# A mixture-of-experts kernel: the second layer's input is cleared as float32 words on two engines, not as float16 on one

## The chip, the cores and the metric

The kernel runs on one core of a Trainium2 chip. The metric is the device time of one execution in microseconds (us); lower is better. Of the engines, TensorE is called PE in the profile, VectorE DVE, ScalarE ACT, GpSimd POOL, and the queue that issues most DMAs SP.

## The reference, cut to what matters

Three stages follow each other: a linear attention over 4 batches, 8 heads, 768 positions and head size 48; a layer of 8 experts (384 to 1024 to 384) that takes each of the 3072 tokens to the one expert with the largest logit; and a second, dense layer (384 to 2048 to 384).

```python
for t in range(S):                      # attention
    state = alpha[:, :, t, :, None] * state + np.einsum('bhd,bhe->bhde', k[:, :, t], v[:, :, t])
    y[:, :, t] = np.einsum('bhd,bhde->bhe', q[:, :, t], state)
...
for e in range(E):                      # the experts
    mask = expert_idx == e
    h = np.maximum(x[mask] @ w1[e], 0.0)
    out[mask] = gate_w[mask, None] * (h @ w2[e])
...
h = x @ w_in                            # the second layer
g = np.maximum(0.01 * h, h)
return (g @ w_out).astype(np.float32)
```

## The kernel before

Float32 products are made of float16 parts: a value is kept as hi + lo, and a product takes three matmuls (hi·hi, hi·lo, lo·hi).

**Attention and routing** fill the first 235 us. The last thing they do is to scatter the tokens' rows, 128 at a time, into a bucket of rows for each expert in HBM. These scatters are indirect DMAs that POOL issues at L558; the last six leave one after the other, the last at 235.07 us.

**The experts' stage** begins where the attention's pools are closed. Its buffers take the same places in SBUF as those of the attention, so the first instruction that writes to one of them waits until the attention's readers are through, the scatters included (they read the tile `xb`). Two of the new buffers, `x2h` and `x2l`, are the float16 parts of the second layer's input, each [128 partitions, 3, 3504], that is 10,512 float16 numbers on a partition. The experts write their results into them at places that are known only at run time (`ds(ao, CAP)`), each expert 432 columns wide, so both are cleared first:

```python
big = ctx.enter_context(tc.tile_pool(name="big", bufs=1))
x2h = big.tile([P, KD, X2], F16, name="x2h")
x2l = big.tile([P, KD, X2], F16, name="x2l")
nc.gpsimd.memset(x2h, 0.0)          # L698
nc.gpsimd.memset(x2l, 0.0)          # L699
```

The first write of an expert into `x2h` is ACT's at L908, that into `x2l` DVE's at L909, both at the end of the expert's work.

**Expert 0** needs its up to 432 rows as columns. The order of the instructions on each engine is that in which the code emits them. SP fetches the rows from the bucket in four blocks of 128, 128, 128 and 48 (`gather(0)`, L823), then four pieces of weights (L707 and L119), then the rows of expert 1 in two DMAs (`gather(1)`, L820 and L823). The four blocks are then scaled row by row, blocks 0 and 2 on DVE (L744), 1 and 3 on ACT (L742); PE transposes each block in three pieces (L750) into PSUM, and ACT and DVE write the float16 parts of the columns (L70 hi, L71 lo):

```python
def unit_rows(pool, xg, m, on_act=False):               # L738
    xs = pool.tile([P, D], F32, name="xs", bufs=3)
    if on_act:
        nc.scalar.activation(xs[:m], xg[:m, :D], AF.Copy, scale=xg[:m, D:D + 1])
    else:
        nc.vector.tensor_scalar(xs[:m], xg[:m, :D], xg[:m, D:D + 1], None, op0=ALU.mult)
    return xs
...
gather(0)                                               # in the experts' stage
ahead(0)
gather(1)
block_rows(0, 0)                                        # unit_rows on DVE
block_rows(0, 1)                                        # unit_rows on ACT
for n in range(NB):
    if n + 2 < NB:
        block_rows(0, n + 2)
    block_columns(0, n)                                 # L750, L70, L71
```

The matmuls of expert 0 begin with L758 and take all four blocks' columns at once (432). While expert e is computed, the rows of expert e+1 are made ready (L842 and L843, turned to columns by a DMA of ACT's queue, L849), and the weights of expert e+1 and a share of the second layer's are fetched and split into float16 parts (fetches L119 and L707 on SP; the stages on ACT L125, L127, L717 and L723; on DVE L132, L718 to L721 and L725; on POOL L130). The weights of expert 0 were split during the attention.

**The second layer** follows from 519 us on: 6 blocks of 512 tokens, PE busy nearly all the time.

Of the kernel before, what the change touches and what calls it, by code (L numbers as in the profile page):

```python
# [10 lines left out]
F16 = mybir.dt.float16  # L11
F32 = mybir.dt.float32
# [11 lines left out]
NP = H // 2          # head pairs  # L24
NC = S // P          # chunks of a sequence
D = H * HD           # 384
NT = B * S           # 3072 tokens
TT = NT // P         # 24 token tiles
W = P + 1            # a chunk's columns with its pad
AW = NC * W + 1  # L30
KD = D // P          # 3
E, F1, F2 = 8, 1024, 2048
NF1, NF2 = F1 // P, F2 // P
CAP = 432            # tokens of one expert in the static path
NB = -(-CAP // P)
AUG = D + 4          # a bucket row: x, scale in, scale out, token, token
NONE = 4096.0        # no token
CH = 768             # columns of a weight piece
W64 = 384            # of float64
# The engines run in the order of emission: one string for each pair of heads, one letter  # L40
# for each step, as the match statements in body() read them. LAST: the last pair and the
# tokens of the last batch.
# [19 lines left out]
BLK = 512            # columns of one MoE2 block  # L62
NBLK = NT // BLK
X2 = NT + CAP
OVB = 32             # blocks of tokens past the static places, at most


def to_f16_pair(nc, hi, lo, src, scale):
    """hi + lo = scale * src, as float16 parts."""
    nc.scalar.activation(hi, src, AF.Copy, scale=scale)  # L70
    nc.vector.scalar_tensor_tensor(lo, src, scale, hi, op0=ALU.mult, op1=ALU.subtract)  # L71
# [3 lines left out]
def body(ctx, tc, qT, kT, aT, v, emb, tau, w1, w2, w_in, w_out, out):  # L75
# [13 lines left out]
    before = const.tile([P, P], F16, name="before")     # s < t  # L89
# [3 lines left out]
    em8 = const.tile([P, NC, E], F32, name="em8")       # e - 8  # L93
# [5 lines left out]
    row0 = const.tile([P, E], F32, name="row0")         # an expert's first row  # L99
    nc.gpsimd.iota(row0, [[NT, E]], base=0, channel_multiplier=0, allow_small_or_imprecise_dtypes=True)  # L100
    cnt = const.tile([P, E], F32, name="cnt")           # sums over partitions to the row after its last one
    nc.vector.tensor_scalar(cnt, row0, 1.0 / P, None, op0=ALU.mult)
    enT = const.tile([P, KD, E], F32, name="enT")
    n_e = const.tile([P, E], F32, name="n_e")           # tokens of the experts
# [3 lines left out]
    more = []                                           # further pools of stages  # L108
# [36 lines left out]
    class Jobs:  # L145
        """Conversions of weights, each fetched some conversions ahead and done a stage at a time."""
# [9 lines left out]
        def step(self):  # L156
            """The next stage of those under way and the first of one more."""
            self.now = [g for g in self.now if next(g, self) is None]
            if self.got:
                convert, t = self.got.pop(0)  # L160
                g = convert(*t)
                next(g)
                self.now.append(g)
            self.fetch()
# [15 lines left out]
    with tc.tile_pool(name="awk", bufs=2) as awk, \  # L180
# [11 lines left out]
        mask = rt.tile([P, 4, P], F32, name="mask", bufs=1)      # s <= t  # L192
        nc.gpsimd.memset(mask, 1.0)
        nc.gpsimd.affine_select(mask, mask, [[0, 4], [1, P]], ALU.is_ge, 0.0, base=0, channel_multiplier=-1)
        # unit rows of the expert embedding, transposed
# [5 lines left out]
        def norm_of(dst, ssq, tmp, tmp2):  # L201
            """dst = sqrt(ssq): exp(ln / 2) and a Newton step."""
            nc.vector.tensor_scalar(tmp, ssq, 2.0 ** -60, None, op0=ALU.max)
            yield
            nc.scalar.activation(tmp, tmp, AF.Ln)
            nc.scalar.activation(tmp, tmp, AF.Exp, scale=0.5)
            yield 6
            nc.vector.reciprocal(tmp2, tmp)
            yield
            nc.vector.tensor_tensor(tmp2, tmp2, ssq, op=ALU.mult)  # L210
            yield
            nc.vector.tensor_tensor(tmp2, tmp2, tmp, op=ALU.add)
            yield
            nc.vector.tensor_scalar(dst, tmp2, 0.5, 1e-30, op0=ALU.mult, op1=ALU.max)
            yield
# [19 lines left out]
        def tick(at=None):  # L235
            """Two more steps of the chains of small operations; those for the tensor engine where it has the time."""
            for g in 2 * chains:
                if isinstance(g[1], int) and g[1]:
                    g[1] -= 1
                elif g[1] in (0, at):  # L240
                    g[1] = next(g[0], DONE) or 0
            chains[:] = [g for g in chains if g[1] != DONE]
# [9 lines left out]
        # rows that no token takes read as zeros; places without a token say so  # L252
# [16 lines left out]
        # the first two units bring what the rows between heads hold  # L269
# [20 lines left out]
        # one head of the pair each, zeros for the other: written where the head is, never elsewhere  # L290
        qzs = [rt.tile([P, NC, 2, P], F32, name=f"qz{i}", bufs=1) for i in range(2)]
        sts = [rt.tile([P, 2, HD * NC], F32, name=f"st{i}", bufs=1) for i in range(2)]
        # a chunk's whole product of alpha; before the first, none and no sum
# [6 lines left out]
        def prep(i):  # L300
            t = done[i]
            b, hp = units[i]
            if hp == 0:
                xbs[b] = awk.tile([P, NC, AUG], F32, name="xb", bufs=3)
            t.update({n: awk.tile([P, NC, 2 * HD], F16, name=n, bufs=3) for n in ("vh", "vl")})
            # products of alpha from its chunk's start, and one over them
            bc = t["bc"] = awk.tile([P, AW], F32, name="bc", bufs=2)
            nc.vector.tensor_tensor_scan(bc, t["a"], onesP, 0.0, op0=ALU.mult, op1=ALU.add)  # L308
            yield
            bcv = bc[:, 0:NC * W].rearrange("p (c w) -> p c w", w=W)  # L310
            nc.vector.reciprocal(seeds[:, W::W], bcv[:, :, P])
            t["qb"] = awk.tile([P, NC, P], F32, name="qb", bufs=4)
            nc.vector.scalar_tensor_tensor(t["qb"], t["q"].rearrange("p (c w) -> p c w", w=P), 16.0, bcv[:, :, 1:W], op0=ALU.mult, op1=ALU.mult)
            yield
            rc = awk.tile([P, AW], F32, name="rc", bufs=1)
            nc.vector.tensor_tensor_scan(rc[:, ::-1], t["a"][:, ::-1], seeds[:, ::-1], 0.0, op0=ALU.mult, op1=ALU.add)  # L316
            yield
            t["kh"] = awk.tile([P, NC, P], F32, name="kh", bufs=3)
            nc.vector.scalar_tensor_tensor(t["kh"], t["k"].rearrange("p (c w) -> p c w", w=P), 16.0,
                                           rc[:, 1:1 + NC * W].rearrange("p (c w) -> p c w", w=W)[:, :, 1:W], op0=ALU.mult, op1=ALU.mult)  # L320

# [4 lines left out]
        def values(i, eng=nc.gpsimd):  # L326
            """The pair's v, scaled, and its float16 parts."""
# [35 lines left out]
        def part(i, eng):  # L363
            """The float16 parts of the next of the masked scores."""
# [9 lines left out]
        def turns(*gs):  # L374
            """Steps of generators, one of each in turn."""
            gs = list(gs)
            while gs:
                gs = [g for g in gs if next(g, DONE) != DONE]
                tick()
# [29 lines left out]
        def combine(i, g):  # L409
            """Half of the chunks, in steps."""  # L410
# [52 lines left out]
        def last_columns(b, c0, n):  # L463
            """The last of the columns and logits of n tiles."""
# [9 lines left out]
        def scales(b, c0=0, n=NC):  # L474
            """The norms of the rows of n tiles, and what follows from them."""
            xb, cs, lo = xbs[b], slice(c0, c0 + n), 2 * (NP - 1) * HD
            ssq, t0, t1, nrm, ls, r = (rts[b][0][:, i, cs] for i in range(6))
            if n < NC:
                # the last pair's columns
# [15 lines left out]
        def route(b, scaled, c0=0, n=NC):  # L495
            """Experts, places and gates of the tokens in n tiles of batch b."""
# [14 lines left out]
            # the first expert that holds the maximum  # L511
# [15 lines left out]
            # an expert's first row and the tokens before this one at its expert  # L527
# [13 lines left out]
            # the gate: the largest probability  # L541
# [19 lines left out]
        with tc.manual_schedule():  # L561
# [9 lines left out]
            toward = []                         # tiles whose squares are to come  # L571
            for i in range(NU - 1):
                br, step = divmod(i - 5, NP)        # the batch whose tokens are routed
# [60 lines left out]
            # the last pair of heads and the last batch's tokens, by halves  # L634
# [63 lines left out]
    nc.gpsimd.memset(x2h, 0.0)  # L698
    nc.gpsimd.memset(x2l, 0.0)  # L699
# [10 lines left out]
    def convert_piece64(raw, hi, lo, n):  # L710
        """From the bits of float64: pairs of words, the low one first."""
# [4 lines left out]
        # 23 bits of the significand under the exponent less 896, then the sign (0 of a zero)  # L716
# [10 lines left out]
    def second_jobs(e):  # L727
        """This expert's share of the second layer's weights."""
# [9 lines left out]
    def unit_rows(pool, xg, m, on_act=False):  # L738
        """m bucket rows, scaled to unit length."""
# [69 lines left out]
    with tc.tile_pool(name="mx", bufs=2) as mxp, tc.tile_pool(name="mh", bufs=1) as mhp, \  # L809
# [26 lines left out]
        def block_pair(e, n):  # L836
            """A block's unit rows in float16 parts."""
# [7 lines left out]
        def block_turn(e, n):  # L845
            """To columns, on the way from one tile to the other."""
# [9 lines left out]
        with tc.manual_schedule():  # L856
            tiles = [w_first] + [[] for _ in range(E)]

            def ahead(e):
                """What runs while expert e is computed."""  # L860
# [51 lines left out]
    more.clear()  # L912
    with tc.tile_pool(name="gp", bufs=1) as gp, tc.tile_pool(name="gs", bufs=3) as gs, \
# [6 lines left out]
        def past_static():  # L920
            """The blocks of 128 tokens past an expert's static places: their rows and experts."""
# [106 lines left out]
```

## Time and profile before

| | us |
|---|---|
| median of three runs (lowest, highest) | 902.45 (898.48, 906.56) |
| span of the profiled execution, first to last instruction | 900.2 |
| PE busy in that span | 771.4 |
| DVE / ACT / POOL busy | 524.1 / 406.6 / 268.6 |
| mean clock granted to PE | 0.92 |

The span is one execution on the chip, read by the hardware profiler; the median of the runs stands 2.25 us above it. Busy time is the time in which an engine had an instruction under way, so an instruction that is held up by another engine counts as busy. In the rows below an engine's idle time stands in brackets with what ended it.

### The profile page before, as it was taken

Reading aid. Unit: us, or ns where it says so; the run is one execution under the profiler, and the core shown is the slowest. Engines: PE = TensorE matmul, PEld = TensorE weight load, DVE = VectorE, ACT = ScalarE, POOL = GpSimd, SP = SyncE. Lnnn points to the kernel's source line nnn. Section 1 sums busy time; section 2 is a strip of 40 time slices with the busy share of each in tenths; the row PEclk is TensorE's granted clock in tenths of the full one; section 3 lists DMA queues with packets and bytes.
Section 4 is the critical chain, followed back from the end, with each engine's and each line's share of the span. In section 5 each row is a group of like instructions: output and inputs, shape, how many; then the busy total and the mean of one; then the engine's idle time right before and its main releaser. Section 6 shows DMA issues by size and latency. Waiting matters only on the chain.

```text
span 900.2 us, 12570 instructions
## 1 busy us (share of the span) xinstructions
PE 771.4 (86%) x4757; PEld 464.0 (52%) x4757; DVE 524.1 (58%) x846; ACT 406.6 (45%) x763; POOL 268.6 (30%) x199
## 2 busy tenths in 40 slices
PE   4777688869069888988779899999999999999996
PEld 3667577758034444444334445545546546455453
DVE  8999999995577566666566674062260350440620
ACT  4555555545036675665666343152250340431520
POOL 6866765765633322322323000100000001001001
PEclk9888876877569998999989999999999999999999
DMA  9886653312435758769857000000000000000000
GB/s 222 237 206 192 154 164 111 88 33 89 169 89 173 169 137 241 149 160 231 132 168 211 19 3 9 27 1 15 22 1 18 18 1 27 10 9 25 2 10 29
DMA packets 64338, 84.86 MB, mean 94 GB/s; under 512 B 30664, under 2 KB 44880, under 8 KB 64272
## 3 DMA queue, kind: packets, MB, share of 16 engines
q1 hardware_dynamic: 42096, 69.85, 29.6%
q10 hardware_dynamic: 19040, 4.65, 3.1%
q0 software_dynamic: 3136, 9.50, 2.8%
q8 instruction: 39, 0.64, 0.3%
q14 instruction: 27, 0.22, 0.1%
HBM read 62.66 MB, written 14.91 MB: 86 GB/s over the span
## 4 chain that ended last, share of the span: by engine, by line
issue 41%; DVE 25%; DMA 13%; PE 11%; ACT 5%; POOL 4%; SPq 0%; DVEq 0%; ACTq 0%; POOLq 0%
DMA wstage<-in_w_out 6%; DVE bc L308 3%; DVE rc L316 3%; POOL out L806 3%; DMA xt<-xs 3%; DVE t L719 2%; DVE a L359 2%; DMA meta<-xg 2%; DVE st L406 2%; ACT wstage L125 2%; DVE xs L744 2%; DVE w2l L132 1%; DMA a<-in_aT 1%; PE yp L426 1%; ACT w2h L127 1%
## 5 line engine op out<-in xcount | busy, mean ns | idle before, releaser
L789 DVE SCALAR_TENSOR_TENSOR g<-ps,r 128x512 f32<-128x512 f32 x96 | 65.6, 684 | 150.3 <-ACT r L788 150.3
L806 POOL DMA_INDIRECT out<-osb,tki x24 | 23.5, 980 | 350.7 <-ACT osb L805 350.7
L801 PE MATMUL ps<-woh,gh 128*128 128x384 f16 x384 | 125.2, 326 | 0.0
L802 PE MATMUL ps<-wol,gh 128*128 128x384 f16 x384 | 125.2, 326 | 0.0
L803 PE MATMUL ps<-woh,gl 128*128 128x384 f16 x384 | 125.2, 326 | 0.0
L783 PE MATMUL ps<-x2h,wih 128*128 128x512 f16 x288 | 109.2, 379 | 0.0
L785 PE MATMUL ps<-x2h,wil 128*128 128x512 f16 x288 | 109.2, 379 | 0.0
L784 PE MATMUL ps<-x2l,wih 128*128 128x512 f16 x288 | 109.1, 379 | 0.0
L793 DVE TENSOR_TENSOR gl<-g,gh 128x512 f16<-128x512 f32 x96 | 66.4, 692 | 64.1 <-ACT gh L792 64.0
L792 ACT ACTIVATE gh<-g 128x512 f16<-128x512 f32 x96 | 60.4, 629 | 83.8 <-DVE g L789 83.8
L372 POOL TENSOR_TENSOR al<-a,ah 128x512 f16<-128x512 f32 x48 | 73.8, 1548 | 47.7 <-ACT ah L371 47.3
L805 ACT ACTIVATE osb<-ps,ms 128x384 f32<-128x384 f32 x24 | 13.9, 580 | 159.5 <-PE ps L803 159.5
L758 PE MATMUL ps<-xt,w1h 128*128 128x432 f16 x192 | 68.7, 358 | 20.1 <-DVE hl L764 19.1
L773 PE MATMUL ps<-hl,w2h 128*128 128x432 f16 x192 | 68.2, 355 | 12.2 <-DVE hl L764 11.9
L772 PE MATMUL ps<-hh,w2h 128*128 128x432 f16 x192 | 68.3, 356 | 3.5 <-ACT hh L763 3.4
L130 POOL TENSOR_TENSOR w1l<-wstage,w1h 128x768 f16<-128x768 f32 x24 | 39.8, 1658 | 98.0 <-ACT w1h L127 97.9
L759 PE MATMUL ps<-xt,w1h 128*128 128x432 f16 x192 | 68.6, 357 | 0.0
L760 PE MATMUL ps<-xt,w1l 128*128 128x432 f16 x192 | 68.6, 357 | 0.0
L774 PE MATMUL ps<-hh,w2l 128*128 128x432 f16 x192 | 68.2, 355 | 0.0
L349 PE MATMUL sc<-qz,kh 128*128 128x256 f32 x192 | 61.9, 476 | 3.9 <-DVE a L359 1.6
L130 POOL TENSOR_TENSOR w2l<-wstage,w2h 128x768 f16<-128x768 f32 x24 | 40.6, 1704 | 73.6 <-ACT w2h L127 73.5
L788 ACT ACTIVATE r<-ps 128x512 f32<-128x512 f32 x96 | 55.9, 583 | 8.2 <-PE ps L785 8.2
(199 smaller groups left out, 1512.6 us busy)
## 6 DMA issues: line engine op xcount, KB each, us to landing
wstage<-in_w SPq DMA_DIRECT2D x64, 384.0 KB, 5.2
wstage<-in_w_in SPq DMA_DIRECT2D x16, 384.0 KB, 3.2
wstage<-in_w_out SPq DMA_DIRECT2D x16, 384.0 KB, 7.1
bucket<-zero SPq DMA_DIRECT2D x8, 582.0 KB, 6.1
xg<-bucket SPq DMA_DIRECT2D x7, 582.0 KB, 8.1
a<-in_aT SPq DMA_DIRECT2D x28, 145.3 KB, 3.0
q<-in_qT SPq DMA_DIRECT2D x28, 144.0 KB, 3.6
k<-in_kT SPq DMA_DIRECT2D x28, 144.0 KB, 3.8
```

What stands on the lines that cost most here:

```text
L130: nc.gpsimd.tensor_tensor(lo, st, hi, op=ALU.subtract)
L372: eng.tensor_tensor(lo, m, hi, op=ALU.subtract)
L758: nc.tensor.matmul(ps, w1h[:, k, fs], xth[:, k], start=k == 0, stop=False)
L759: nc.tensor.matmul(ps, w1h[:, k, fs], xtl[:, k], start=False, stop=False)
L760: nc.tensor.matmul(ps, w1l[:, k, fs], xth[:, k], start=False, stop=k == KD - 1)
L772: nc.tensor.matmul(ps, w2h[:, f, dsl], hh, start=f == 0, stop=False)
L783: nc.tensor.matmul(ps, wih[:, k, fs], xh[:, k], start=k == 0, stop=False)
L784: nc.tensor.matmul(ps, wih[:, k, fs], xl[:, k], start=False, stop=False)
L785: nc.tensor.matmul(ps, wil[:, k, fs], xh[:, k], start=False, stop=k == KD - 1)
L801: nc.tensor.matmul(ps, ghs[f][:, ts], woh[:, f], start=f == 0, stop=False)
L802: nc.tensor.matmul(ps, ghs[f][:, ts], wol[:, f], start=False, stop=False)
L803: nc.tensor.matmul(ps, gls[f][:, ts], woh[:, f], start=False, stop=f == NF2 - 1)
```

## The change

`x2h` and `x2l` are cleared as float32 words, half as many elements for the same bytes, and the clearing of `x2h` goes from GpSimd to VectorE. Nothing else is changed (comments that are left out in the changed file make no instruction).

```diff
     x2h = big.tile([P, KD, X2], F16, name="x2h")
     x2l = big.tile([P, KD, X2], F16, name="x2l")
-    nc.gpsimd.memset(x2h, 0.0)
-    nc.gpsimd.memset(x2l, 0.0)
+    nc.vector.memset(x2h.rearrange("p k t -> p (k t)").bitcast(F32), 0.0)
+    nc.gpsimd.memset(x2l.rearrange("p k t -> p (k t)").bitcast(F32), 0.0)
```

On DVE, at the passage from attention to experts (L691 is the last small operation of the routing; the names in brackets are the counters that an instruction waits for, DMASW those of the DMAs that POOL issues, DMAHW those of SP's and ACT's queues, eight of each, taken in turn):

```order
 L690 TENSOR_TENSOR ohs<-ohs,n_e 128x1 [waits DVE_49] x7
 L691 CAST offi<-ohs 128x8 [waits DVE_49]
-L744 TENSOR_SCALAR xs<-xg 128x384 [waits DMASW7_49,DMAHW0_49,DMASW6_49,DMAHW1_49,DMASW5_49,DMAHW3_49,DMASW4_49,DMAHW4_49,DMASW1_49,DMAHW5_49,DMASW0_49,DVE_49]
+L698 MEMSET x2h 128x5256 [waits DMASW6_49,DMASW7_49,DMASW5_49,DMAHW0_49,DMASW4_49,DMAHW1_49,DMASW1_49,DMAHW3_49,DMASW0_49,DMAHW4_49,DVE_49,Pool_49]
+L744 TENSOR_SCALAR xs<-xg 128x384 [waits DMAHW5_49]
```

The clearing of `x2h` now stands ahead of both L744 on DVE and takes over their wait for the six last scatters (DMASW 4 to 7, 0 and 1); L744 itself waits for its rows alone (DMAHW5).

On POOL, at the same place, between the last scatters and the first conversion of expert 1's weights:

```order
 L558 DMA bucket<-xb,sloti 24576x388 [waits DMASW2_49]
 L558 DMA bucket<-xb,sloti 24576x388 [waits DMASW3_49]
-L698 MEMSET x2h 128x10512 [waits DMASW7_49,DMAHW0_49,DMASW6_49,DMAHW1_49,DMASW5_49,DMAHW2_49,DMASW4_49,DMAHW3_49,DMASW1_49,DMAHW4_49,DMASW0_49,DMAHW5_49,DVE_49,DMAHW6_49,PE_49,DMAHW7_49,Activation_49,Pool_49]
-L699 MEMSET x2l 128x10512
+L699 MEMSET x2l 128x5256 [waits DMASW7_49,DMAHW0_49,DMASW6_49,DMAHW1_49,DMASW5_49,DMAHW2_49,DMASW4_49,DMAHW3_49,DMASW1_49,DMAHW4_49,DMASW0_49,DMAHW5_49,DVE_49,DMAHW6_49,PE_49,DMAHW7_49,Activation_49,Pool_49]
 L130 TENSOR_TENSOR w1l<-wstage,w1h 128x768 [waits Activation_49] x3
 L130 TENSOR_TENSOR w2l<-wstage,w2h 128x768 [waits Activation_49] x3
```

One memset of 5,256 elements stands where two of 10,512 stood, with the same wait ahead of it.

On ACT, while expert 0 is computed, the instructions stay as they were and some counters that they wait for change:

```order
 L842 ACTIVATE xs_2724<-xg 128x384
-L849 DMA_TRANSPOSE xt_2632<-xs_2683 128x6x128 [waits DMAHW2_49,DVE_49]
+L849 DMA_TRANSPOSE xt_2632<-xs_2683 128x6x128 [waits DMAHW4_49,DVE_49]
 L723 ACTIVATE wih<-t_2687 128x384 [waits DVE_49,Pool_49]
-L125 ACTIVATE wstage<-wstage 128x768
+L125 ACTIVATE wstage<-wstage 128x768 [waits DMAHW2_49]
```

Such differences stand in what runs beside experts 0, 1 and 2, on ACT, DVE, SP and PE, and nowhere later.

## Rows read from the trace of the kernel before

**Rows 1.** The page: the clock granted to TensorE in 40 slices, tenths of full.
```profile
PEclk9888876877569998999989999999999999999999
```

**Rows 2.** The chain that ended last: start us, us, what (x pieces).
```profile
240.51 15.80 DVE xs L744 x2
256.36 0.92 PE ps L750 x3
```

**Rows 3.** Timeline, 235 to 262 us: start, us, engine line op, [idle before <-releaser].
```profile
238.08 1.76 SPq L823 DMA_DIRECT2D xg<-bucket  x4
238.22 8.86 POOL L698 MEMSET x2h<- 128x10512 f16 x1 [2.20 <-DMA bucket<-xb,sloti]
...
240.51 15.79 DVE L744 TENSOR_SCALAR xs<-xg 128x384 f32<-128x384 f32 x2 [7.87 <-DMA xg<-bucket]
...
247.02 9.07 POOL L699 MEMSET x2l<- 128x10512 f16 x1
...
247.50 1.51 PE L750 MATMUL ps<-ident,xs 128*128 128x128 f32 x6 [16.65 <-DVE xs L744]
...
248.80 0.60 ACT L742 ACTIVATE xs<-xg 48x384 f32<-48x384 f32 x1
...
256.36 1.39 PE L750 MATMUL ps<-ident,xs 128*128 128x128 f32 x6 [7.34 <-DVE xs L744]
...
258.12 0.52 PE L758 MATMUL ps<-xt,w1h 128*128 128x432 f16 x1 [0.38 <-ACT xt L70]
...
262.08 0.35 PE L760 MATMUL ps<-xt,w1l 128*128 128x432 f16 x1
...
262.15 0.61 ACT L842 ACTIVATE xs<-xg 128x384 f16<-128x384 f32 x1
```

**Rows 4.** Line 744: its instructions, min/median/max ns, first and last start.
```profile
L744 DVE TENSOR_SCALAR xs<-xg x2: 6780/7933/9086, 240.5 to 247.2; 128x384 f32<-128x384 f32 x2
```

**Rows 5.** Groups by form over the span: busy us, mean ns, idle before.
```profile
L296 POOL MEMSET qz<- 128x1536 f32 x2 | 2.7, 1405 | 0.0
...
L718 DVE TENSOR_SCALAR t<-wstage 128x384 uint32<-128x384 uint32 x32 | 11.3, 355 | 18.3 <-DMA wstage<-in_w_out 18.2
...
L296 POOL MEMSET bend<- 128x288 f32 x3 | 0.9, 364 | 0.0
...
L188 DVE MEMSET onesP<- 128x775 f32 x1 | 0.7, 704 | 1.0 <-PEq L1018 1.0
```

**Rows 6.** Timeline of the first microseconds, DVE and POOL.
```profile
1.03 0.70 DVE L188 MEMSET onesP<- 128x775 f32 x1 [1.03 <-PEq L1018]
1.18 0.28 POOL masks.py:199 TENSOR_SCALAR_AFFINE_SELECT ident<-ident 128x128 f32<-128x128 f32 x1
...
1.43 0.28 POOL L92 TENSOR_SCALAR_AFFINE_SELECT before<-ones 128x128 f16<-128x128 f16 x1
...
1.84 0.70 DVE L191 MEMSET seeds<- 128x775 f32 x1
```

**Rows 7.** DMA issues of 237.9 to 239.85 us: KB each, us to landing.
```profile
xg<-bucket SPq DMA_DIRECT2D x3, 194.0 KB, 3.0
xg<-bucket SPq DMA_DIRECT2D x1, 72.8 KB, 3.7
```

**Rows 8.** DMA issues of 242.8 to 243.9 us, the next expert's rows.
```profile
xg<-bucket SPq DMA_DIRECT2D x1, 582.0 KB, 8.1
```

**Rows 9.** Stretches: length, busy us of each engine, granted clock, DMA share, GB/s.
```profile
260.00:261.80 1.80, 1.80 (x6) 0.76 (x5) 0.00 (x0) 0.08 (x1) 0.00 (x0) 0.50 0.00 0
262.50:264.00 1.50, 1.50 (x10) 0.82 (x9) 1.47 (x4) 1.14 (x4) 0.00 (x0) 1.00 0.00 0
```

**Rows 10.** Waits of all engines, 258 to 519 us.
```profile
PE ps L758 <- DVE hl L764: 19.1, 10, 5.1
DVE t L718 <- DMA wstage<-in_w_out: 18.2, 5, 6.3
```

## The prediction

> **What bounds the kernel now.** I read the chain that ended last first, since it names the places where time can be won at all. Most of its pieces are short; the reader is to look for the few long ones, and one of the longest is a pair of DVE instructions: L744, 15.80 us for two scalings of a 128x384 block [rows 2]. No DVE instruction of that size should need so long: L718, with the same shape, 4-byte elements and one source in SBUF, has a mean of 355 ns [rows 5]. So the next view is line 744 by itself: 6,780 and 9,086 ns, starts at 240.5 and 247.2 [rows 4]. The timeline says what lies beside them: POOL clears x2h from 238.22 for 8.86 us, that is to 247.08, and x2l from 247.02 for 9.07 us, to 256.09; the first L744 ends at 240.51 + 6.78 = 247.29, the second at 240.51 + 15.79 = 256.30 [rows 3]. Each scaling ends 0.2 us after a memset of POOL, whenever it began. I read this as the scaling standing still while POOL writes, so the "busy" DVE is waiting.
>
> What hangs on it is PE. It idles 16.65 us ahead of its first transposes and 7.34 us ahead of the second group, both times released by L744, and the first matmul of expert 0 stands at 258.12 [rows 3]. The row of PE's clock shows the same hole: the eleventh and twelfth slices (225 to 270 us) are at 5 and 6 tenths, and from then on nearly all are at 9 [rows 1]. From 258 us on PE is the engine that is waited for, so a start that is earlier there should move the end by as much.
>
> **The change part by part.**
>
> *POOL, removed and shortened.* Two memsets of 10,512 elements become one of 5,256. What counts is the number of elements, not the bytes: float32 memsets of POOL take 1,405 ns for 1,536 and 364 ns for 288 elements [rows 5], that is (1405 - 364) / (1536 - 288) = 0.834 ns for one more element, and the float16 ones start 247.02 - 238.22 = 8.80 us apart, 0.837 ns for each of 10,512 [rows 3]. So 5,256 words cost 4.4 to 4.5 us; POOL is through at 238.2 + 4.5 = 242.7 in place of 256.1. The wait ahead of it is the old one.
>
> *DVE, added.* A memset of 5,256 words stands before both L744, with the wait for the last scatters that L744 had. SP's fetch and POOL's memset, which wait for the same scatters, begin at 238.08 and 238.22 [rows 3], so it begins at 238.2 too. DVE is idle there (7.87 us before 240.51, [rows 3]), so the first 2.3 us of it are free; the rest is queued ahead of the scalings and so of PE. Its price: the row of a 775-word memset has 704 ns, but the next one starts 1.84 - 1.03 = 0.81 us after it [rows 6], and the distance is what the next instruction sees. By the row 5,256 x 0.908 = 4.8 us, by the distance 5,256 x 1.045 = 5.5 us; I take 5.5. The trace has no DVE memset of an even count in SBUF; if such a one went at twice the pace, it would take 2.7 us, and POOL's 242.7 would decide. DVE is free at 238.2 + 5.5 = 243.7.
>
> The Trainium skill (PSUM — Partial Sum Buffer, Specifications (TRN2)) timed a VectorE memset at 1.04 ns for an element on trn2 from the rows around it, because the memset's own row does not tell its length. The distance above agrees with it (1.045), the row's 704 ns does not; by the row alone the forecast would be 0.7 us lower.
>
> *Whether the two memsets can run side by side.* In the first microseconds they do: while DVE clears 775 words from 1.03 to 1.73, POOL's selections start at 1.18 and 1.43 and take 0.28 us each [rows 6], and neither side is stretched. I take no cost. The other end is that one waits for the other: 4.5 us (a rival below).
>
> The Trainium skill (SBUF — State Buffer, Who interferes with whom) has a rule that separates the cases: a DVE instruction with at most one SBUF input shares nothing with GpSimd unless it runs in a mode that uses the second port pair, and a copy or scaling in such a mode blocks fully until GpSimd's instruction ends. L744 agrees with its second half (6.78 and 9.09 us in place of 0.36); by its first half the sum is the forecast's, were the memset in such a mode, the rival's.
>
> *What is late next.* Both scalings then go at their own length, 0.36 us each by L718: the first ends at 243.7 + 0.36 = 244.1. Its block is there by 240.5, where it ended DVE's wait; the other two full blocks and the 48-row one take 3.0 us (median) and 3.7 us from issue, the last being issued before 239.84 [rows 3, 7], so all are there by 243.6. PE follows 0.2 us after the scaling (247.29 to 247.50), at 244.3. Six transposes take 1.51 us, and from the start of the second six to L758 it was 258.12 - 256.36 = 1.76 us [rows 3]: L758 at 244.3 + 1.5 + 1.8 = 247.6. ACT's scaling of the last block came 248.80 - 247.50 = 1.3 us after PE's start and takes 0.60; so it ends at 246.2, before the last three transposes are due (244.3 + 9 x 0.25 = 246.6). Won: 258.1 - 247.6 = 10.5 us.
>
> *The clock.* PE's first matmuls of expert 0 run at a granted clock of 0.50, the lower level, and at 262.5 it is 1.00 [rows 9]; the row at 262.08 is 0.35 us long where that at 258.12 had 0.52 [rows 3]. About 3.8 us pass at half speed, so at most 1.9 us can come back. Before, PE did six transposes, rested 7.3 us, and did six more; now it does twelve and the matmuls without a rest, so the rise may come earlier in the matmuls. Ends 0 and 1.9; I take 0.8, nearer to the row as it is.
>
> *What does not move.* The first consumer of expert 1's rows, L842, stands 262.15 - 258.12 = 4.0 us behind L758, so at 251.6; these rows were issued by 242.9 at the latest and took 8.1 us [rows 8], landing by 251.0, still in time, though with under 1 us left. That fetch does not depend on DVE or POOL, so it does not come earlier. The first writes into x2h and x2l come at the end of expert 0, long after the memsets.
>
> *Sum.* 10.5 + 0.8 = 11.3 us: 900.2 - 11.3 = 888.9 for the span. The runs' median lies 2.25 us above the profiled span, so 902.45 - 11.3 = 891.1.
>
> **The rivals.**
>
> *One memset waits for the other.* If DVE's even-count memset contends with POOL's as L744 did, the second starts at 242.7 and ends, at DVE's full 5.5 us, at 248.2, 4.5 us later than above: 11.3 - 4.5 = 6.8 won, 895.6. For it: L744's two rows [rows 4]. Against it: the overlap of [rows 6], with an odd count.
>
> *The gain is taken back in the experts' stage.* DVE waits 18.2 us for weights (L718 on the fetched pieces, five times) [rows 10], and expert 1's rows come barely in time. If fetches rather than PE set the first experts' pace, half of the gain is lost: 11.3 / 2 = 5.6 won, 896.8. Against it: fetches are issued as places come free, and these come free earlier too; and PE's own waits there are for DVE's hl, 19.1 us, not for weights [rows 10].
>
> *Slower: other counters.* In what runs beside experts 0, 1 and 2 some instructions now wait for a different DMA counter. If this puts a transposing or fetching DMA behind a longer one, each of the three stages can lose as much as the longest wait for a piece of weights, 6.3 us [rows 10]: 3 x 6.3 - 11.3 = 7.6 slower, 910.0. From 11.3 / 3 = 3.8 us a stage it decides. Against it: the counters change, the queues' order does not.
>
> **How the numbers follow.** Forecast 0.76, memsets in turn 0.12, gain half lost 0.08, slower 0.04. A measurement of this kernel can tell about 1% (9.0 us) from no change. The forecast, 11.3, clears that by 2.3 us, and the three runs of before lie 4.0 below and 4.1 above their median, so some of its chance falls within 1% (0.03), while the two middle cases, 6.8 and 5.6, give as much back: faster 0.76, within 1% 0.20, slower 0.04. Range: down from 891.1 by the memset at twice its pace (1.0), the full clock (1.1) and 3.5 for the runs, 885.5; up to 895.6 and 896.8 with a part of the runs' spread, 898.5.
>
> **What would show it.** The chain without a long L744; L744 of under 0.5 us each; DVE's memset from 238.2 to about 243.7 and POOL's to 242.7, side by side; L758 near 247.6; the second layer (L783) beginning as much earlier as L758 does. Wrong: a memset or L744 that begins or ends with the other engine's memset; L758 early but the second layer not.

## The result, and the profile after

| | before | changed |
|---|---|---|
| median of nine runs each, us (lowest, highest) | 901.25 (898.48, 906.56) | 894.14 (890.59, 896.22) |
| ratio of the times, 95% interval | | 0.9909 [0.9881, 0.9938] |
| span of the profiled execution, us | 900.2 | 892.6 |
| busy, us: PE / DVE / ACT / POOL | 771.4 / 524.1 / 406.6 / 268.6 | 777.1 / 516.2 / 406.5 / 254.5 |

The changed kernel is 0.9% faster, 7.1 us by the medians. A second comparison of the same two kernels (below) gave 10.0 us. The forecast was 891.1 us, a gain of 11.3 us. Of all the runs below two were in a slower state, one of the kernel before (912.01 us) and one of *words, both on POOL* (1,543.52 us); the ratios leave them out, the medians do not.

The chain that ended last in the changed kernel, from the end of the last scatter on (start us, us, what), with what answers to [rows 2]:

```profile
240.90 1.17 issue
242.07 4.44 DVE x2h L698
246.50 0.23 DVE xs L744
...
246.93 0.89 PE ps L750 x3
...
257.87 6.84 DMA xt<-xs
264.74 0.62 ACT xs L842
```

The 15.80 us of L744 have become 0.23, behind a clearing of x2h on DVE of 4.44 us with an "issue" of 1.17 us ahead of it. Further on stands a long piece on which the prediction has no row: the DMA that turns the next expert's rows to columns, 6.84 us. The chain of the kernel before has it too, shorter:

```profile
264.78 0.48 DVE t L721
265.26 4.93 DMA xt<-xs
270.22 0.62 ACT xs L842
```

Line 744 by itself in the changed kernel (min/median/max ns, first and last start), which answers to [rows 4]:

```profile
L744 DVE TENSOR_SCALAR xs<-xg x2: 297/352/406, 246.4 to 246.6; 128x384 f32<-128x384 f32 x2
```

The page's row of the clock, which answers to [rows 1], has its hole in the same two slices, the eleventh and twelfth, a little shallower (5 and 7 tenths):

```profile
PEclk9788878677579999998989999999999999999998
```

The timeline of the same stretch as [rows 3]:

```profile
240.97 1.76 SPq L823 DMA_DIRECT2D xg<-bucket  x4
241.11 4.48 POOL L699 MEMSET x2l<- 128x5256 f32 x1 [2.07 <-DMA bucket<-xb,sloti]
242.07 4.44 DVE L698 MEMSET x2h<- 128x5256 f32 x1 [6.41 <-issue]
...
246.42 0.62 DVE L744 TENSOR_SCALAR xs<-xg 128x384 f32<-128x384 f32 x2
...
246.93 2.64 PE L750 MATMUL ps<-ident,xs 128*128 128x128 f32 x12 [13.06 <-DVE xs L744]
...
249.94 0.52 PE L758 MATMUL ps<-xt,w1h 128*128 128x432 f16 x1 [0.38 <-ACT xt L70]
```

The two memsets lie side by side, PE's twelve transposes are one group, and expert 0 starts at 249.94 in place of 258.12. One thing has to be taken out before the two traces are compared: here the last scatter ends 2.9 us later, so SP's first fetch of expert 0's rows, L823, starts at 240.97 in place of 238.08. I call that start F and count from it. L758 stands at F + 20.0 before and at F + 9.0 now, 11.05 us earlier.

ACT's rows behind it show what the long DMA costs:

```profile
264.74 0.61 ACT L842 ACTIVATE xs<-xg 48x384 f16<-48x384 f32 x1 [3.74 <-DMA xt<-xs]
...
275.59 0.53 ACT L908 ACTIVATE x2h<-ps 128x432 f32 x1 [0.30 <-PE ps L774]
```

The same instructions of the kernel before:

```profile
270.22 0.61 ACT L842 ACTIVATE xs<-xg 48x384 f16<-48x384 f32 x1 [1.83 <-DMA xt<-xs]
...
280.68 0.52 ACT L908 ACTIVATE x2h<-ps 128x432 f32 x1
```

The fourth L842 writes into a tile `xs16` of which there are three, so it waits until the first L849 has read its block; ACT, which works in order, stands still for 3.74 us in place of 1.83.

Last the clock (stretch, length, busy us of each engine, granted clock, DMA share, GB/s), which answers to [rows 9]:

```profile
252.00:254.00 2.00, 2.00 (x7) 0.80 (x6) 0.00 (x0) 0.40 (x1) 0.00 (x0) 0.50 0.02 3
254.00:255.00 1.00, 1.00 (x4) 0.44 (x3) 0.84 (x2) 1.00 (x3) 0.00 (x0) 0.50 0.12 17
255.00:256.00 1.00, 1.00 (x6) 0.47 (x5) 0.97 (x3) 0.07 (x1) 0.00 (x0) 0.84 1.01 61
256.00:258.00 2.00, 2.00 (x13) 1.07 (x12) 1.86 (x5) 1.22 (x3) 0.00 (x0) 1.00 0.67 115
```

PE is busy without a rest and stays at the lower level until 255.3, 5.4 us after L758; before it was 3.8 us.

### The profile page after: what moved, and what is told of

Same layout as the page of the kernel before. It is cut to its first block, busy times and chain, and to the rows that moved or that the text cites. A ratio compares the mean times of both kernels' runs of the same rounds, so it can differ in the third digit from the quotient of the medians.

```text
span 892.6 us, 12571 instructions
## 1 busy us (share of the span) xinstructions
PE 777.1 (87%) x4757; PEld 468.0 (52%) x4757; DVE 516.2 (58%) x847; ACT 406.5 (46%) x763; POOL 254.5 (29%) x198
## 4 chain that ended last, share of the span: by engine, by line
issue 40%; DVE 20%; PE 16%; DMA 14%; ACT 4%; POOL 4%; SPq 0%; ACTq 0%; POOLq 0%; DVEq 0%
DMA wstage<-in_w_out 5%; DMA xt<-xs 3%; DVE rc L316 3%; POOL out L806 3%; PE sc L349 3%; DVE bc L308 2%; DVE a L359 2%; ACT wstage L125 2%; DVE st L406 2%; PE yp L426 1%; DVE t L719 1%; DVE w2l L132 1%; DMA a<-in_aT 1%; PE ps L784 1%; PE ps L783 1%
## 5 line engine op out<-in xcount | busy, mean ns | idle before, releaser
L806 POOL DMA_INDIRECT out<-osb,tki x24 | 23.5, 980 | 350.7 <-ACT osb L805 350.7
L783 PE MATMUL ps<-x2h,wih 128*128 128x512 f16 x288 | 109.2, 379 | 0.0
L372 POOL TENSOR_TENSOR al<-a,ah 128x512 f16<-128x512 f32 x48 | 71.5, 1499 | 49.8 <-ACT ah L371 49.7
L758 PE MATMUL ps<-xt,w1h 128*128 128x432 f16 x192 | 69.7, 363 | 15.7 <-DVE hl L764 15.2
L773 PE MATMUL ps<-hl,w2h 128*128 128x432 f16 x192 | 68.6, 357 | 12.7 <-DVE hl L764 12.5
L759 PE MATMUL ps<-xt,w1h 128*128 128x432 f16 x192 | 69.9, 364 | 0.1
L426 PE MATMUL yp<-st,qb 128*128 128x96 f32 x160 | 39.0, 390 | 30.5 <-DVE st L406 30.5
```

The lines of the kernel that those rows point to most:

```text
L372: eng.tensor_tensor(lo, m, hi, op=ALU.subtract)
L758: nc.tensor.matmul(ps, w1h[:, k, fs], xth[:, k], start=k == 0, stop=False)
L759: nc.tensor.matmul(ps, w1h[:, k, fs], xtl[:, k], start=False, stop=False)
L783: nc.tensor.matmul(ps, wih[:, k, fs], xh[:, k], start=k == 0, stop=False)
```

## The experiments

The theory so far: the stall of L744 is gone as forecast (11.05 us at L758), and about 2.7 us of that are lost again before ACT's first L908 (the mean of two pairs, the second of them below), by the clock and by ACT's wait for the transposing DMA. The rivals: that the later F belongs to the change; that the clock alone takes the loss; that DVE's memset is as long as its row says; that any way of freeing L744 gives the same.

All times from F, in us. L849 is the first of its kind, L842 the fourth, L908 the first; "lead" is how long before that L849 the rows of expert 2 (`gather(2)`, L820) were issued (negative: behind it); "DMA" is the time from that L849 to the fourth L842, left out where that L842 did not wait for it. "none" is a fetch that was put behind all four L849.

| kernel | L758 | L849 | lead | DMA | L842 | L908 | median | ratio to before [95%] |
|---|---|---|---|---|---|---|---|---|
| before | 20.0 | 27.2 | 0.5 | 5.0 | 32.1 | 42.6 | 901.25 | |
| before, again | 20.0 | 27.2 | 0.5 | 5.3 | 32.5 | 43.0 | 905.13 | 1.0000 [0.9968, 1.0032] |
| changed | 9.0 | 16.9 | 0.2 | 6.9 | 23.8 | 34.6 | 894.14 | 0.9909 [0.9881, 0.9938] |
| changed, again | 9.0 | 17.3 | 0.3 | 6.4 | 23.7 | 34.2 | 892.54 | 0.9877 [0.9834, 0.9919] |
| words, both on POOL | 11.3 | 19.4 | 1.5 | 4.1 | 23.5 | 34.0 | 896.83 | 0.9917 [0.9884, 0.9950] |
| words, both on DVE | 14.5 | 21.6 | 0.4 | 5.3 | 27.0 | 37.4 | 897.29 | 0.9934 [0.9903, 0.9965] |
| before, scalings on ACT | 7.1 | 14.2 | -4.9 | | 21.3 | 31.5 | 890.39 | 0.9844 [0.9805, 0.9884] |
| changed, put_meta(0) later | 9.0 | 17.2 | -1.0 | 7.6 | 24.8 | 35.7 | 895.98 | 0.9861 [0.9821, 0.9902] |
| changed, rows late | 9.0 | 16.5 | none | 4.0 | 20.6 | 31.1 | 894.38 | 0.9856 [0.9816, 0.9896] |
| before, rows late | 20.0 | 27.4 | none | | 30.5 | 41.0 | 905.51 | 0.9979 [0.9950, 1.0007] |
| changed, fourth buffer | 9.0 | 16.0 | -0.5 | | 19.0 | 28.7 | 884.67 | 0.9788 [0.9754, 0.9821] |
| before, fourth buffer | 20.0 | 27.8 | 1.1 | | 30.8 | 40.5 | 896.86 | 0.9926 [0.9893, 0.9959] |
| changed, scalings on ACT, fourth buffer | 7.4 | 15.9 | -0.5 | | 18.9 | 28.9 | 885.16 | 0.9787 [0.9751, 0.9824] |

Each ratio is against the kernel before on the same chip. Its median there was 902.5 us for "again" and "words" (one set), 902.5 for the four kernels with a fourth buffer or the scalings on ACT (one set), 907.5 for put_meta(0) and 907.8 for the two with rows late (one set); medians are compared within a set alone, else ratios, and a ratio need not be the quotient of the two medians. Apart from the first pair a kernel has 4 to 12 runs; the kernel before, measured twice in one set, gave 902.5 and 905.1, so a difference of medians is uncertain by 2 to 3 us.

**Both kernels once more.** No edit.

> The kernel before, once more, for a second profile. Let F be the start of SP's first fetch of expert 0's rows (238.08 us before, 240.97 us after). Theory (chance): the routing's end moves from execution to execution with the clock, by some us, so F may come out anywhere from 235 to 242 us, and F to the first matmul of expert 0 is again 20.0 us (within 0.3). Rival (the change makes the attention 2.9 us longer): F is 238.1 within 0.5.

> The changed kernel once more. F to the first matmul of expert 0 was 8.97 us and should be 9.0 again, so 11.0 us less than before. Theory (chance in F): F comes out anywhere from 235 to 242 us, and over all runs the time is 9 to 11 us under the kernel before (ratio 0.988 to 0.990). Rival (the attention is longer in this kernel): F is 241.0 within 0.5 and the time is 7 to 8 us under (ratio 0.991 to 0.992).

F was 242.31 in the kernel before and 239.06 in the changed one: the order of the first pair is turned round. The later F is chance, not the change; over all thirteen profiles of this study F lies between 238.08 and 245.05. From F to L908 the pair gains 42.95 - 34.16 = 8.8 us, the first pair 42.60 - 34.62 = 8.0.

**Float32 words, both memsets on POOL** (the edit against the changed kernel).

```diff
-    nc.vector.memset(x2h.rearrange("p k t -> p (k t)").bitcast(F32), 0.0)
+    nc.gpsimd.memset(x2h.rearrange("p k t -> p (k t)").bitcast(F32), 0.0)
```

> Float32 words alone, both memsets still on GpSimd. Theory (the scaling on VectorE stands still while GpSimd writes, and a memset costs by elements): the memsets take 4.45 us each, the first scaling ends at F + 4.8, the second at F + 9.3, and the first matmul of expert 0 stands at F + 11.0, 9 us earlier than before; the time is 8 to 9 us under before. Rival (a memset costs by bytes, the engine is what matters): two of 8.9 us, F + 20, the time of before.

The timeline of this kernel:

```profile
242.92 4.48 POOL L698 MEMSET x2h<- 128x5256 f32 x1 [2.06 <-DMA bucket<-xb,sloti]
...
245.33 6.90 DVE L744 TENSOR_SCALAR xs<-xg 128x384 f32<-128x384 f32 x2 [7.88 <-DMA xg<-bucket]
...
247.34 4.69 POOL L699 MEMSET x2l<- 128x5256 f32 x1
```

L744 is stretched again: its two instructions end at 252.23, 0.2 us after POOL's second memset (252.03). So it is POOL's writing that holds L744, not that DVE had no memset. Half the elements alone bring L758 8.7 us forward; moving one half to DVE adds 2.3 us. But at the fourth L842 that advantage is gone (23.5 against 23.8), and the two ratios cannot be told apart. The time was expected 8 to 9 us under the kernel before; it is 5.7 us under by the medians.

**Float32 words, both memsets on DVE** (against the changed kernel).

```diff
-    nc.gpsimd.memset(x2l.rearrange("p k t -> p (k t)").bitcast(F32), 0.0)
+    nc.vector.memset(x2l.rearrange("p k t -> p (k t)").bitcast(F32), 0.0)
```

> Float32 words, both memsets on VectorE, none on GpSimd. Theory (a memset of 5,256 words holds VectorE for 5.4 us, though its row says 4.44): the first scaling starts 10.9 us after F (5.45 in the changed kernel), each takes 0.3 to 0.4 us, and the first matmul of expert 0 stands at F + 14.4; the time is 5.5 us under before. Rival (the row is right, 4.44 us each, and something else held the scaling back for 1 us): scaling at F + 9.9, matmul at F + 13.4.

Its timeline:

```profile
240.74 1.76 SPq L823 DMA_DIRECT2D xg<-bucket  x4
241.84 4.44 DVE L698 MEMSET x2h<- 128x5256 f32 x1 [6.50 <-issue]
...
247.32 4.44 DVE L699 MEMSET x2l<- 128x5256 f32 x1 [1.04 <-issue]
...
251.67 0.62 DVE L744 TENSOR_SCALAR xs<-xg 128x384 f32<-128x384 f32 x2
```

The rows of the memsets have 4.44 us, yet the second starts 5.48 us after the first, with 1.04 us of "issue" that no row fills, and L744 follows at F + 10.93. A memset of 5,256 words holds DVE for 5.5 us. The Trainium skill (PSUM — Partial Sum Buffer, Specifications (TRN2)) gives 1.04 ns for an element of a VectorE memset of 2-byte elements into PSUM, timed from the rows around it; 5.48 us over 5,256 words in SBUF is 1.04 ns too.

**The four scalings on ACT, the memsets as before** (against the kernel before; the argument is `on_act`).

```diff
-            ... min(P, CAP - n * P), e == 0 and n % 2)
+            ... min(P, CAP - n * P), e == 0)
```

> The kernel before with its two float16 memsets on GpSimd, all four blocks of expert 0 scaled on ScalarE and none on VectorE. Theory (only VectorE's scaling is stopped by GpSimd's writes): GpSimd still writes from F + 0.1 to F + 18, ScalarE's scalings take 0.6 us each, and the first matmul of expert 0 stands at F + 6.9 (20.04 before, 8.97 changed). Of these 13 us part is given back beside the unmoved fetch: the first write into x2h at F + 33.5 to 34, no earlier than in the changed kernel; the time is within 1 us of the changed kernel's. Rivals: GpSimd's writes slow ScalarE too (matmul at F + 9 or later); nothing is given back (L908 at F + 30).

Its timeline:

```profile
245.19 8.86 POOL L698 MEMSET x2h<- 128x10512 f16 x1 [2.13 <-DMA bucket<-xb,sloti]
247.73 0.61 ACT L742 ACTIVATE xs<-xg 128x384 f32<-128x384 f32 x1 [11.14 <-DMA xg<-bucket]
...
252.12 0.52 PE L758 MATMUL ps<-xt,w1h 128*128 128x432 f16 x1 [0.38 <-DVE xt L71]
...
253.99 8.85 POOL L699 MEMSET x2l<- 128x10512 f16 x1
...
258.21 0.62 DVE L843 SCALAR_TENSOR_TENSOR xs<-xg,xs 128x384 f16<-128x384 f32 x1 [1.18 <-ACT xs L842]
258.75 4.31 DVE L718 TENSOR_SCALAR t<-wstage 128x384 uint32<-128x384 uint32 x1
```

This separates the engines. While POOL writes, ACT's scaling of the same shape keeps its 0.61 us, so what stops L744 is not the memory but something that DVE and POOL share. DVE's next instruction of L744's kind, L718, stands for 4.31 us, from 258.75 to 263.06, and POOL's second memset ends at 253.99 + 8.85 = 262.84; L718 has a mean of 355 ns [rows 5]. Yet POOL's writing does not stop every instruction of DVE: L843, of the same shape but with two inputs in SBUF, takes its 0.62 us in the middle of it. What is held here are the TENSOR_SCALAR instructions, L744 and L718. The Trainium skill (SBUF — State Buffer, Who interferes with whom) names a pair of ports that DVE and GpSimd share and says that ACT waits for nobody. The two rows agree with the second; that it is ports that are shared, no run here shows by itself.

The stall of L744 is thus avoided with the long float16 memsets still on POOL, and this kernel is no slower than the changed one: 11.3 us are won at L908 against the two runs of before (mean 42.8). At L758 it was 13.0. The recorded expectation, L908 at F + 33.5 to 34 because of the fetch, missed by 2 us: `gather(2)` left 4.9 us behind the first L849 here, and no L842 waited for that DMA. What took a part of the 13.0 is L718's stall, as the waits of all engines from 255 to 275 us show (engine, tile, line, waited for: us, times, longest):

```profile
ACT wih L723 <- DVE t L721: 4.7, 2, 4.3
...
PE ps L758 <- DVE hl L764: 2.9, 1, 2.9
```

ACT waits 4.3 us for the chain of DVE that L718 begins, and PE, behind it, 2.9 us.

**put_meta(0) later.** What lengthens the transposing DMA? The first idea was a fetch of weights, L119, which stands at F + 13.2 in both kernels and so comes to lie beside the transposes when these come earlier. It waits in SP's queue behind the write of expert 0's token places, `put_meta(0)`. With that write one step of the loop later, the fetch goes ahead of it:

```diff
-                    if f == 2:
+                    if f == (2 if e else 3):
```

> The changed kernel with expert 0's places (L829, L831) written one step later, so that the fifth fetch of weights (L119) goes to SP right behind the rows of expert 1, at about F + 7, and no longer behind L831 at F + 13.2. Theory (that fetch, unmoved at F + 13.2 and landing 5.2 us later, lies beside the DMA transposes now that these start at F + 17): with it away, the first transpose lands 5.0 to 5.4 us after its issue (6.4 and 6.9 in the changed kernel), the fourth block of L842 stands at F + 22.3 (23.7) and L908 at F + 33 (34.4). Rival (the next fetch and the rows of expert 2, which move with the stage, hold the transposes up by themselves): 6.5 us, F + 23.7 and F + 34.4 as before.

The idea fell. One of the two fetches of L119 now left at 245.13, F + 5.9, and the DMA became longer, 7.6 us, L908 later (35.7). SP's waits from 241 to 272 us say why (engine, line, waited for: us, times, longest). In the kernel before:

```profile
SPq L119 <- DVE t L719: 12.7, 1, 12.7
SPq L831 <- DMA meta<-xg: 5.2, 1, 5.2
```

In the changed kernel:

```profile
SPq L831 <- DMA meta<-xg: 5.2, 1, 5.2
SPq L119 <- DVE t L719: 1.6, 1, 1.6
...
SPq L820 <- DMA meta<-xg: 1.0, 1, 1.0
```

With put_meta(0) later:

```profile
SPq L831 <- DMA meta<-xg: 6.3, 1, 6.3
SPq L820 <- DMA meta<-xg: 2.6, 1, 2.6
```

`gather(2)` (L820 and L823, 655 KB) overwrites the buffer that `put_meta(0)` (L829 and L831) reads, and so waits for those writes to land. `put_meta(0)` hangs on SP's own sequence and on its first write (L831 waits 5.2 us for that of L829 in both kernels): L831 leaves at F + 12.7 or 12.8 and lands at F + 16.7. Before, `gather(2)` came ten microseconds later, at F + 26.7, held by DVE's use of a weight buffer (12.7 us). Now everything else is early, and the write's landing is what it waits for:

```profile
257.64 0.38 SPq L820 DMA_DIRECT2D xg<-bucket  x1
```

That is F + 16.7, at the same moment as the first L849 at F + 16.9; with put_meta(0) later it leaves at F + 18.3, a microsecond behind the first L849. The second idea: the DMA that turns a block is slow when this fetch goes out beside it.

**gather(2) behind the transposes.** The rows of expert 2 are fetched three steps later, in the changed kernel and in the one before:

```diff
-                    if f == 4 and e + 2 < E:
+                    if f == (4 if e else 7) and e + 2 < E:
```

> The changed kernel with the fetch of expert 2's rows (L820, L823) moved, beside expert 0 alone, behind one more fetch of weights (L707), which waits for POOL until about F + 27. Theory (that fetch of 655 KB cannot leave before the write of expert 0's places, L831, has landed at F + 16.7, which did not move, and so now leaves together with the first DMA transpose at F + 17, where in the kernel before it had left 0.5 us ahead; it is what holds the transpose up): the first transpose lands 2.5 to 3.5 us after its issue (6.4 and 6.9 in the changed kernel), the fourth block of L842 stands at F + 20 and L908 at F + 29 to 30 (34.4); the time is 3 to 5 us under the changed kernel. Rival (the weights' fetches hold it up): landing 6 us or more, L908 at F + 34.

> The kernel before with the same fetch moved behind L707. Theory: the first transpose lands in 2.5 to 3.5 us there too (5.0 and 5.3), L908 at F + 40.5 (42.8), 11 us behind the changed kernel with the same edit. Rival: L908 stays at F + 42.8.

In the changed kernel the DMA fell from 6.9 and 6.4 us to 4.0, and L908 came 3.3 us earlier from F than in the mean of the two changed runs (34.4), 0.6 of it ahead of L849. The direction is the theory's, the sizes fall short of it (a DMA of 2.5 to 3.5 us, L908 at F + 29 to 30). In the kernel before the fourth L842 no longer waits at all, 3.1 us after the first L849, by ACT's timeline:

```profile
272.73 0.61 ACT L842 ACTIVATE xs<-xg 128x384 f16<-128x384 f32 x1
...
275.49 0.61 ACT L842 ACTIVATE xs<-xg 48x384 f16<-48x384 f32 x1
```

What the transposing DMAs took from issue to landing stands among the rows of the tile `xt` (min/median/max of the first four). In the kernel before:

```profile
DMA to landing us min/median/max: 2.3/2.5/4.9
```

In the changed one:

```profile
DMA to landing us min/median/max: 2.3/2.5/6.8
```

With put_meta(0) later:

```profile
DMA to landing us min/median/max: 2.3/2.5/7.6
```

The longest of the four is the first, the one beside the fetch; the others take 2.3 to 2.5 us in all three. In the changed kernel with the rows late (not every landing is on record there):

```profile
DMA to landing us min/median/max: 2.6/3.3/4.0
```

Over the kernels of the table with three buffers and the scalings on DVE the DMA grows as the lead shrinks: 4.1 us at a lead of 1.5, 5.0 to 5.3 at 0.4 to 0.5, 6.4 and 6.9 at 0.3 and 0.2, 7.6 where the fetch is issued a microsecond behind. So the second idea holds for what is above 4.0 us. These 4.0 the changed kernel has without that fetch too, 1.5 more than the other three DMAs take in the changed kernel; where they come from was not tried. In the whole time the pair of this experiment differs by 905.51 - 894.38 = 11.1 us, the forecast's size; whether the changed kernel itself is faster by it (0.9856 against 0.9909 and 0.9877) stays open, as the intervals meet.

**A fourth buffer.** The other way to take the wait from ACT:

```diff
-            xs[n] = mxp.tile([P, 2, D], F16, name="xs16", bufs=3)[:m]
+            xs[n] = mxp.tile([P, 2, D], F16, name="xs16", bufs=4)[:m]
```

> The changed kernel with a fourth buffer for the scaled rows of the next expert (xs16), so that their fourth block no longer waits for the first DMA transpose. F is the start of SP's first fetch of expert 0's rows. Theory (the earlier start brings the transposes beside a fetch of weights that did not move, they take 6.4 to 6.9 us in place of 5.0 to 5.3, ACT waits for them in order and gives part of the gain back): the fourth block of L842 stands near F + 20 (23.7 without the buffer) and the first write into x2h (L908) near F + 31.8 (34.4 without); the time is 2 to 3 us under the changed kernel. Rival (the loss in expert 0 is that of the slower clock alone): L908 stays at F + 34 and the time stays.

> The kernel before with the same fourth buffer. Theory: its fourth block waits 1.8 to 2.2 us for the transpose, so the first write into x2h comes at F + 40.8 (42.6 and 43.0 without), first matmul of expert 0 at F + 20.0 as before; 9 us behind the changed kernel with the buffer, where without it the two are 8.4 apart. Rival (the wait is no cost in the kernel before): F + 42.8.

ACT's timeline in the changed kernel with it:

```profile
259.77 0.60 ACT L842 ACTIVATE xs<-xg 48x384 f16<-48x384 f32 x1
...
269.44 0.52 ACT L908 ACTIVATE x2h<-ps 128x432 f32 x1
```

No wait stands ahead of the fourth L842, and L908 is at F + 28.7. That is 5.7 us earlier than in the mean of the two changed runs, 1.1 of it ahead of L849, and more than expected (F + 31.8, the time 2 to 3 us under the changed kernel). The buffer serves all seven turns of rows to columns, not that beside expert 0 alone: in the kernel before it wins 2.3 us at L908 and 5.6 us in the median. With the buffer the change is worth 40.51 - 28.65 = 11.9 us at L908 and 896.86 - 884.67 = 12.2 us in the median, so once ACT does not wait for that DMA the gain at L758 reaches L908 whole and shows in the medians: 11.05, and 0.8 more because the clock in these two profiles rose 5.1 and 3.4 us after L758. The changed kernel with four buffers, 884.67 us, beats both kernels. The transposing DMAs still take long beside the fetch (up to 6.6 us, and 8.2 in the next kernel), but no L842 waits for them.

**All of it together:** the changed kernel with the four scalings on ACT and four buffers.

> The changed kernel with all four blocks scaled on ScalarE and with the fourth buffer. Theory: first matmul of expert 0 at F + 6.9, fourth block of L842 at F + 18, first write into x2h at F + 30; the time is 12 us under the kernel before, 4 under the changed kernel, and under both single edits. Rival (the DMAs beside expert 0 set its end whatever is done on ACT): L908 at F + 32 or later.

885.16 us, the same as without the scalings on ACT, where less than either single edit was expected. L758 comes 1.6 us earlier from F, but the first L849 does not (15.9 and 16.0): in this profile PE stayed at the lower clock for 6.4 us after L758, in the other for 3.4.

## Why the prediction was right, and where its sizes were wrong

The direction and the mechanism held, the time lies in the range, and the gain was forecast too high: 11.3 us against 8.4 from F to L908 (mean of two pairs) and 7.1 and 10.0 in the medians. That the time came within 3.0 us of the forecast is in part luck: the gain was 4.2 us short, and the base, the median of three runs, lay 1.2 us above that of nine. Whether the gain clears the 1% that the prediction drew is not decided: the two ratios give 0.9% and 1.2%, and both intervals reach over it.

*POOL and the stall.* POOL's memset took 4.48 us (4.4 to 4.5), each L744 0.30 and 0.41 (0.36), and POOL's writing is what had held L744: shown by words_pool, where the stretch comes back, and by the scalings on ACT, where it goes with POOL's work unchanged.

*DVE's memset.* 5.5 us, by the distance between starts and not by the row, was right: L744 follows F by 5.45 us. The row would have made the forecast 0.7 us too good.

*Side by side.* The two memsets overlap from 242.07 to 245.59 and keep their lengths, so the rival in which they take turns fell.

*L758.* 11.05 us earlier from F, 10.5 forecast. The working put it 9.5 us after F, it came at 9.0: half of the difference by L750, half because twelve transposes and what follows took 3.0 us and not 3.3.

*The clock* is a term with the wrong sign. The prediction took +0.8, on the thought that PE's twelve transposes without a rest would bring the rise earlier. It came 5.4 and 6.1 us after L758, against 3.8 in both profiles of before; half of the 1.6 and 2.3 us more is 0.8 and 1.1, and the first L849 is indeed only 10.1 us earlier from F (mean of the two pairs), 1.0 less than L758. I would not call it an effect of the change: over the thirteen profiles the rise came 3.4 to 6.4 us after L758, late (5.9) in words_pool, where PE did rest between its transposes, and early (3.4) in the changed kernel with four buffers, where it did not. The term should have been zero with about a microsecond on either side.

*"What does not move"* is the step that failed, and with it the sentence that an earlier start of PE moves the end by as much. It followed expert 1's rows to their scaling and stopped there. The next instruction in the chain of before was the transposing DMA, 4.93 us, and a fetch that is held by SP's own sequence came to stand beside it: another 1.5 us lost between L849 and the fourth L842, and 0.2 behind it. 11.05 - 1.0 - 1.5 - 0.2 = 8.4.

*The rival "gain taken back in the experts' stage"* (half lost) was right in kind and wrong in place and size: a quarter was lost (2.7 of 11.05) up to L908, about 1.0 by the clock and 1.5 not by weights on DVE but by ACT's wait for a buffer. The waits of all engines from 250 to 511 us of the changed kernel, which answer to [rows 10] (18.2 and 19.1), have not grown:

```profile
PE ps L758 <- DVE hl L764: 15.2, 10, 4.8
DVE t L718 <- DMA wstage<-in_w_out: 14.9, 5, 5.3
```

*Slower by other counters* was not seen.

*The profiled spans* differ by 900.2 - 892.6 = 7.6 us. That is 11.05 of L758, less 2.89 of F, which is chance, less 0.6 for all the rest. The loss was 3.1 us at L908 in this pair, so 2.5 of it came back later.

*The second layer* was to begin as much earlier as L758. Its line in the kernel before:

```profile
L783 PE MATMUL ps<-x2h,wih x288: 378/379/379, 518.3 to 860.2; 128*128 128x512 f16 x144
```

In the changed kernel:

```profile
L783 PE MATMUL ps<-x2h,wih x288: 378/379/379, 510.6 to 852.5; 128*128 128x512 f16 x144
```

From F that is 280.2 and 269.6 us, 10.6 earlier and close to what was forecast; in the second pair it is 274.6 and 269.3, 5.3 earlier. Over the thirteen profiles the way from the first L908 to the first L783 took 230.3 to 239.6 us, and that from there to the end 381.9 to 382.0. So the loss up to L908 is shown, and what the other seven experts make of it is not: they vary by more than the loss, from a cause that was not followed.

## What to carry to other kernels

Where a small DVE instruction has a duration that ends with a GpSimd one, look whether it is a wait; here it was one, and it could be removed on either side: fewer elements on GpSimd, or the work on an engine that GpSimd did not hold up. A gain at the head of a stage must be followed down the chain of waits to the next buffer that is handed back: what is paced by another queue (here a write of SP, 12.7 us after the fetch) does not come earlier with it, and can then collide with what does. One more buffer at the place where ACT waited for a DMA was worth about as much in the changed kernel (from 0.9909 and 0.9877 to 0.9788) as the change itself.

## What was not expected of the hardware

- A DVE memset's row is 1.04 us shorter than the time that it holds the engine (4.44 against 5.48 for 5,256 words) and begins that much late, with "issue" as the idle time; on POOL row and distance agree (4.48 and 247.34 - 242.92 = 4.42).
- A GpSimd memset of 4.5 to 9 us held a DVE TENSOR_SCALAR of 0.3 to 0.4 us until it ended (L744, L718), but neither an ACT scaling of the same shape (0.61 us) nor DVE's L843 with two inputs in SBUF (0.62 us).
- The DMA that turns the first block of rows landed after 4.9 and 6.8 us where a fetch of 655 KB was issued half a microsecond and less ahead of it, and after 7.6 us where the fetch came a microsecond behind; the other three in these traces took 2.3 to 2.5 us. Without the fetch the first still took 4.0 us in the changed kernel, and was through within 3.1 us in the one before.
- The start of the experts' stage varied by 7 us from run to run, and the clock's rise by 3 us: single profiles of one kernel are compared from a common event, not from zero.
